# First expert's rows by one-hot products from rows kept on chip, gates applied to its outputs, and a fourth buffer for split q and k

## The chip, the cores and the metric

One Trainium2 chip, one core. The metric is device time in microseconds of one launch. A core has TensorE (PE, matrix products; its weight loads are listed as PEld), VectorE (DVE), ScalarE (ACT), GpSimd (POOL) and SyncE (SP, which here issues transfers); each runs its own instructions in order and they meet by semaphores.

## The reference

Attention for 2 batches, 8 heads, 576 positions, width 64, with a bias from a small network of the positions; a mixture of experts over the 1152 resulting rows; and a gated network over its output. What matters here is the middle part:

```python
logits = x @ w_gate
expert_idx = np.argmax(logits, axis=1)
...
gate_w = probs[np.arange(N), expert_idx]
...
for i in range(N):
    e = expert_idx[i]
    if counts[e] < capacity:
        disp[e, counts[e]] = x[i]
        pos[i] = counts[e]
        counts[e] += 1
        keep[i] = True
h = np.maximum(np.einsum('ecd,edf->ecf', disp, w1), 0.0)
y = np.einsum('ecf,efd->ecd', h, w2)
...
        out[i] = gate_w[i] * y[expert_idx[i], pos[i]]
```

x has 1152 rows of 512, there are 8 experts of 512 x 1024 x 512, and the capacity is 288.

## The kernel before

All large products are done in a 32-bit type that TensorE reads in one pass (fp32r), each operand split into a high part (a copy rounded to that type) and a low part (the rest): high by high, high by low, low by high.

**Attention.** The work is a list of units, nine per head: four tiles of 128 queries of batch 0, one tile of the last 64 queries of both batches, four tiles of batch 1. For each head and batch `load` (line 217) brings q, k and v in one transfer (`raw`, two buffers), and GpSimd splits them: high parts of q and k (L231, two instructions of 640 columns), low part of q (L233), low part of k (L235, the tile K2), high and low part of v (L240, L242). The tiles QK and K2 have three buffers, so a split waits until TensorE is done with the head before last. `LOADS0` and `LOADS` give the units at which the two loads of the next head are issued. Softmaxed scores are multiplied with v; `folds` (L399) turns a head's output by one product per token tile into rows, with the eight gate logits beside them; VectorE divides by the sums (L411), SyncE stores the 64 columns of all 1152 rows into `rows` in device memory (L413), and GpSimd adds up the logits in `lg` (L417, L419).

**Routing.** `route` (L605) works on the 1152 x 8 logits with some thirty small VectorE instructions and a few products. It gives `slot` (L699): for each row its place in the experts' order of size, largest first, counted from a base below zero so that only kept rows match; and then ranks, lists and registers (L702 to L715).

**Experts.** `experts` (line 1062) takes the largest expert first (k = 0, up to 288 rows), then the second. For k = 0: `pick` (L870) makes nine one-hot tiles of 128 tokens x 288 slots in 16 bits, `gather` (L889 to L902) multiplies them with the tokens' numbers and gates (27 products with nine columns each) to get a list of row numbers, and loads these rows from `rows` by three indirect transfers on GpSimd's queue. Then `scale` multiplies each row by its gate, `turn` transposes on TensorE (L937), and ScalarE and VectorE split into `dh` and `dl` (L941, L942). `split` (L962, L963) does the same for the expert's weights, eight pieces of 1024 columns; the first three are loaded as soon as the largest expert is known. `full` (L975) then runs 4 x 24 products for the first layer (L992), with high and low parts of the hidden values (L996, L997), 4 x 24 for the second (L1006), and `evac` writes the outputs' high and low parts into `x2h` and `x2l` (L969, L970), from which the gated network (`swiglu`) reads. Within `full` the steps `around` and `extra` put the next expert's loads, splits and gather, and the narrowing of the gated network's 64-bit weights (L769 to L775), between the pieces. The columns of `x2h` and `x2l` past the first 288 are zeroed by ScalarE (L1152, eight instructions) between routing and the experts. `warm` (L1141) issues products that nobody reads: 16, 12 and 64 of them.

The order on each engine is that in which the code is written (`manual_schedule`); nothing is reordered by a scheduler in the parts shown.

Of the kernel before, what the change touches and what calls it, by code (L numbers as in the profile page):

```python
# [23 lines left out]
NT = 9  # L24
# [26 lines left out]
LOADS0, LOADS = (0, 7), (0, 5)  # L51
# [15 lines left out]
WARM = (16, 12, 64)  # L67
# [77 lines left out]
def build(tc, ins, out, cap):  # L145
    nc = tc.nc
    cap = max(0, min(int(cap), N))
    with ExitStack() as ctx:
# [18 lines left out]
        x_p = ctx.enter_context(tc.tile_pool(name="axh", bufs=2))  # L167
        with ExitStack() as pctx:
            ps = pctx.enter_context(tc.tile_pool(name="ps", bufs=2, space=PSUM))
            attention(tc, ins, cst, rt, lg, x_p, rows, tids, out, ps)  # L170
        moe(tc, ins, cst, cap, rt, lg, x_p, rows, tids, out)


def attention(tc, ins, cst, rt, lg, x_p, rows, tids, out, ps):
    nc = tc.nc
    with ExitStack() as ctx:
# [26 lines left out]
        with ExitStack() as actx:  # L203
            attn_phase(tc, actx, (load, qk, loads), cst, (bias, head), (out, zi), fold, lg, x_p, rows, ps)


def loader(tc, ctx, ins):
# [3 lines left out]
    qk_p = ctx.enter_context(tc.tile_pool(name="aqk", bufs=3))  # L211
# [36 lines left out]
def attn_phase(tc, ctx, load, cst, bias, zeros, fold, lg, x_p, rows, ps):  # L248
# [14 lines left out]
    sco, ex, tp, tt, sums, pt, ot, rsum = {}, {}, {}, {}, {}, {}, {}, {}  # L263
    eps = m_p.tile([128, 1], F32, name="eps", bufs=1)
    V.memset(eps, 1e-9)

# [132 lines left out]
    def folds(h):  # L399
# [5 lines left out]
        for t0, tn in ((0, 5), (5, 4)):  # L405
# [6 lines left out]
            if t0:  # L412
# [71 lines left out]
    assert not pt and not ot  # L484

# [248 lines left out]
def moe(tc, ins, cst, cap, rt, lg, x_p, rows, tids, out):  # L734
# [3 lines left out]
    with ExitStack() as ctx:  # L738
        xp = ctx.enter_context(tc.tile_pool(name="x2", bufs=1))
        x2h = xp.tile([128, 4, XC], F32R, name="x2h")  # L740
        x2l = xp.tile([128, 4, XC], F32R, name="x2l")
# [47 lines left out]
        with ExitStack() as bctx:  # L789
            bctx.enter_context(tc.manual_schedule(engines=ENGINES))  # L790
            kept, rare = experts(tc, bctx, ins, cst, cap, rt, lg, x_p, rows, tids, x2h, x2l, load64, narrow, split)
# [27 lines left out]
class Experts:  # L819


    def __init__(self, tc, ins, cst, rt, pool, pp, x_p, rows, tids, x2h, x2l):
# [23 lines left out]
        self.hl = pool.tile([128, 8, SL], F32R, name="hl")  # L846
        self.eid, self.base = {}, {0: 0}
# [26 lines left out]

    def gather(self, k, few=False):

# [3 lines left out]
        if k == 1:  # L880
            pl = [pp.tile([128, SL], F32, name="pl", tag="py0", bufs=1)]
        else:
            pl = [pp.tile([128, 512], F32, name="pl", tag="ph") for r in range(npart if k == 0 else 1)]
# [486 lines left out]
```

## Time and profile before

| | us |
|---|---|
| median of 3 runs | 447.68 |
| lowest, highest | 446.14, 449.28 |
| profiled execution, its own time | 446.49 |
| its span | 444.6 |
| bias and head 0 | to about 80 |
| heads 1 to 7 | to about 220 |
| routing to the first expert's products | 220 to 243.4 |
| first and second expert | 243.4 to about 302 |
| rest of the experts, gated network | to the end |

Stages and waits are read from one profiled execution, whose times are from the start of its span. Busy time counts instructions, not waiting; the granted clock of TensorE is given as a share of its full level, 2.4 GHz, and the lower level is half of it.

### The profile page before, as it was taken

What the parts mean: (1) busy time and instruction counts of PE and PEld (TensorE: products, weight loads), DVE (VectorE), ACT (ScalarE), POOL (GpSimd) and SP (SyncE); (2) the same over time, 40 slices, a digit from 0 to 9 for tenths busy, and PEclk for the clock granted to TensorE, in tenths of its full rate; (3) what the DMA queues carried; (4) which work ended last, traced back from release to release, by engine and by line L of the source; (5) the groups of instructions that cost most, each with busy time, mean ns of one, the idle gap of its engine ahead of it and who ended that gap; (6) DMA issues with size and microseconds to landing.
All of it is one profiled execution on the core that took longest, in us unless ns stands there. A gap on an engine that the chain in (4) does not pass through costs nothing.

```text
span 444.6 us, 8757 instructions
## 1 busy us (share of the span) xinstructions
PE 396.1 (89%) x3122; PEld 342.5 (77%) x3122; DVE 343.1 (77%) x737; ACT 279.1 (63%) x586; POOL 115.5 (26%) x109
## 2 busy tenths in 40 slices
PE   8786777679999999999986989998989999999993
PEld 5332236569999999998865988996978888888992
DVE  6999987379999999999675578854778888787341
ACT  4888887479989989889591448444354444444221
POOL 0000000898597888960021100010000000000003
PEclk9999899899999999999988899999999999999999
DMA  7555557872955857720294988985444444440003
GB/s 252 206 214 190 183 192 226 269 260 82 287 184 187 241 179 244 232 97 6 57 308 31 331 253 125 351 238 181 143 142 143 142 143 142 143 143 1 1 1 116
DMA packets 54210, 76.35 MB, mean 172 GB/s; under 512 B 16562, under 2 KB 35762, under 8 KB 54160
## 3 DMA queue, kind: packets, MB, share of 16 engines
q1 hardware_dynamic: 51744, 70.62, 50.0%
q0 software_dynamic: 800, 2.48, 3.2%
q10 hardware_dynamic: 1616, 2.62, 1.9%
q8 instruction: 26, 0.43, 0.4%
q14 instruction: 24, 0.20, 0.1%
HBM read 59.13 MB, written 16.59 MB: 170 GB/s over the span
## 4 chain that ended last, share of the span: by engine, by line
PE 44%; DVE 21%; ACT 10%; issue 6%; DMA 5%; POOL 2%; SPq 0%; DVEq 0%; POOLq 0%; ACTq 0%
PE pg L1243 9%; PE tp L334 6%; PE po L381 5%; PE sc L282 5%; PE ph L992 5%; PE py L1006 4%; DVE swl L785 4%; DVE wf L771 4%; PE po L408 3%; DMA bias<-biasd 2%; DVE sg L1251 2%; ACT pth L337 2%; PE pb L569 2%; DMA xr<-rows,ri 2%; ACT ex L314 2%
## 5 line engine op out<-in xcount | busy, mean ns | idle before, releaser
L297 DVE CUSTOM_DVE_ANT_0 ex<-sc,bias 128x576 f32<-128x576 f32 x72 | 53.8, 748 | 9.3 <-PE tt L344 7.0
L231 POOL TENSOR_TENSOR QK<-raw,zero 128x640 fp32r<-128x640 f32 x28 | 34.5, 1254 | 90.6 <-DMA raw<-in_qkv 87.2
L569 PE MATMUL pb<-r,w 128*32 128x288 f32 x576 | 45.2, 424 | 14.4 <-ACT r L563 9.4
L565 DVE TENSOR_SCALAR r<-ltab,sl,nb 128x576 f32<-128x576 f32 x116 | 57.2, 570 | 0.0
L314 ACT ACTIVATE ex<-ex,mx 128x576 f32<-128x576 f32 x72 | 55.8, 775 | 1.4 <-DVE mx L297 0.7
L337 ACT ACTIVATE pth<-tp 128x512 fp32r<-128x512 f32 (+1 forms) x80 | 43.8, 554 | 16.5 <-PE tp L334 7.7
L282 PE MATMUL sc<-QK 128*128 128x288 f32 x160 | 49.1, 324 | 3.6 <-POOL QK L233 3.1
L353 DVE TENSOR_TENSOR ptl<-tp,pth 128x512 fp32r<-128x512 f32 (+1 forms) x80 | 49.6, 628 | 2.3 <-ACT pth L337 1.6
L1243 PE MATMUL pg<-x2h,swh 128*128 128x304 f32 x192 | 46.4, 309 | 4.9 <-DVE sg L1251 4.1
L334 PE MATMUL tp<-cst,ex 128*128 128x128 f32 x288 | 44.6, 278 | 6.2 <-DVE ptl L353 3.8
L569 PEld LDWEIGHTS pb<-r,w 128*32 128x32 f32 x576 | 18.4, 112 | 40.8 <-ACT r L563 22.2
L282 PE MATMUL sc<-K,QK 128*128 128x288 f32 x160 | 45.0, 297 | 1.2 <-POOL K L235 1.2
L1243 PE MATMUL pg<-x2l,swh 128*128 128x304 f32 x192 | 43.9, 303 | 0.0
L381 PE MATMUL po<-pth,W 128*128 128x256 f32 (+1 forms) x145 | 43.6, 321 | 0.0
L1243 PE MATMUL pg<-x2h,swl 128*128 128x304 f32 x192 | 43.6, 301 | 0.0
L1275 POOL DMA_INDIRECT out<-ob,ids x5 | 4.9, 973 | 144.1 <-ACT ob L1272 143.2
L334 PEld LDWEIGHTS tp<-cst,ex 128*128 128x128 f32 x288 | 32.8, 142 | 11.0 <-ACT ex L314 4.6
L1255 ACT ACTIVATE sh<-sg 128x608 fp32r<-128x608 f32 (+1 forms) x13 | 8.8, 673 | 51.2 <-DVE sg L1251 51.2
L1243 PEld LDWEIGHTS pg<-x2h,swh 128*128 128x128 f32 x192 | 32.7, 188 | 9.7 <-DVE sg L1251 7.1
L1251 DVE TENSOR_TENSOR sg<-pg,sg 128x304 f32<-128x304 f32 x48 | 20.7, 468 | 22.1 <-PE pg L1243 18.6
L282 PEld LDWEIGHTS sc<-QK 128*128 128x128 f32 x160 | 30.3, 189 | 5.3 <-POOL QK L233 3.3
L381 PE MATMUL po<-ptl,W 128*128 128x256 f32 (+1 forms) x116 | 33.4, 308 | 0.0
(191 smaller groups left out, 1023.9 us busy)
## 6 DMA issues: line engine op xcount, KB each, us to landing
raw<-in_qkv SPq DMA_DIRECT2D x16, 800.0 KB, 5.7
biasd<-be SPq DMA_DIRECT2D x36, 288.0 KB, 2.2
wr<-in_ew SPq DMA_DIRECT2D x19, 512.0 KB, 8.9
w<-in_mwg SPq DMA_DIRECT2D x12, 512.0 KB, 3.6
w<-in_mwv SPq DMA_DIRECT2D x12, 512.0 KB, 4.7
w<-in_mwo SPq DMA_DIRECT2D x12, 512.0 KB, 6.2
bias<-biasd SPq DMA_DIRECT2D x16, 288.0 KB, 4.1
bias<-biasd SPq DMA_DIRECT2D x17, 256.0 KB, 4.3
```

The source lines that it names most:

```text
L231: P.tensor_tensor(QK[:, o:o + n], raw[:, o:o + n], view(zero, 0, (0, n)), op=ALU.add)
L282: nc.tensor.matmul(sc[:, c, :288], l, K[:, o + c * 288:o + (c + 1) * 288], start=n == 0, stop=n == len(lhs) - 1)
L297: V.tensor_tensor_reduce(e.rearrange("p (c j) -> p c j", c=2), sc[:, :, :288], head[h][:, t].rearrange("p (c j) -> p c j", c=2), scale=-0.125,
L314: A.activation(ex[u], ex[u], AF.Exp, bias=mx, scale=-1.0, accum_out=sums[h][:, col:col + 1])
L334: nc.tensor.transpose(x[:, kt], e[:, kt * 128:(kt + 1) * 128], ident)
L337: A.activation(hi[:, :4, c], x[:, :, o], AF.Copy)
L353: V.tensor_tensor(lo[:, :, c], x[:, :, o], hi[:, :4, c].bitcast(F32), op=ALU.subtract)
L381: nc.tensor.matmul(po[:, :w], W[:, kt], src[:, kt, a:a + w], start=k == 0, stop=k == 8)
L565: V.tensor_scalar(r[g], x, s, nb, op0=ALU.mult, op1=ALU.max)
L569: nc.tensor.matmul(pb[strips[g], c, :288], w2, r[g][:, c * 288:(c + 1) * 288], start=True, stop=True, skip_group_check=True,)
L1243: nc.tensor.matmul(g[:, :TB], w[:, a * 4 + kk], x[:, kk, c0 + b * TB:c0 + (b + 1) * TB], start=kk == 0 and i == 0, stop=kk == 3 and i == 2,)
L1251: V.tensor_tensor(sg[:, cs], g[:, :TB], sg[:, cs], op=ALU.mult)
```

## The change

`x2h` and `x2l` are now made ahead of attention. GpSimd zeroes their columns past 1152 at the start, and after each head `folds` keeps that head's 64 columns of all rows in them, token tiles by 128 partitions, as a high and a low part: on GpSimd for heads 0 to 6, and for head 7 the high part on ScalarE and the low part later on VectorE (`late`). ScalarE's eight zeroing instructions go. `dispatch` makes nine one-hot tiles in fp32r (in the tiles `hh` and `hl`, not yet in use) and multiplies them with the kept rows, 72 products, which gives the first expert's rows transposed, without gate; `halve` is the old end of `turn`. The 27 products for the row numbers and gates of the first expert are still done, its row loads, scaling and transposes are not. `spread` puts the gates into all partitions (three products and a copy), and at the end of the first `full` VectorE multiplies the four output tiles by them. The second expert's gather moves from ahead of `full` to its second piece. QK and K2 get a fourth buffer; head 1's second load is issued at unit 4 of head 0 instead of 7; the warming products are 16 and 24.

```diff
-LOADS0, LOADS = (0, 7), (0, 5)
+LOADS0, LOADS = (0, 4), (0, 5)
...
-WARM = (16, 12, 64)
+WARM = (16, 24)
...
-    qk_p = ctx.enter_context(tc.tile_pool(name="aqk", bufs=3))
+    qk_p = ctx.enter_context(tc.tile_pool(name="aqk", bufs=4))
...
+    for x in x2:
+        nc.gpsimd.memset(x.rearrange("p d c -> p (d c)")[:, NT * DM:].bitcast(F32), 0.0)
+    xhi, xlo = tokens(x2)
...
+                to = slice(h * D, h * D + D)
+                if h == H - 1:
+                    A.activation(xhi[:, :, to], x, AF.Copy)
+                    late.append((xlo[:, :, to], x, xhi[:, :, to].bitcast(F32)))
+                else:
+                    nc.gpsimd.tensor_tensor(xhi[:, :, to], x, view(nil, 0, (0, NT), (0, D)), op=ALU.add)
+                    nc.gpsimd.tensor_tensor(xlo[:, :, to], x, xhi[:, :, to].bitcast(F32), op=ALU.subtract)
...
+    def dispatch(self, late):
+
+        nc, V, rt = self.nc, self.nc.vector, self.rt
+        sel = [self.hh[:, t] for t in range(8)] + [self.hl[:, 0]]
+        for t in range(NT):
+            V.tensor_scalar(sel[t], rt["iota"], rt["slot"][:, t:t + 1], None, op0=ALU.is_equal)
+        V.tensor_tensor(*late, op=ALU.subtract)
+        tp = [self.pp.tile([128, 512], F32, name="etp", tag="ph")[:, :SL] for d in range(4)]
+        x = tokens(self.x2)
+        for dd in (range(3), (3,)):
+            for t in range(NT):
+                for d, n in [(d, n) for n in range(2) for d in dd] if t + 1 < NT else [(d, n) for d in dd for n in range(2)]:
+                    nc.tensor.matmul(
+                        tp[d], x[n][:, t, d * 128:(d + 1) * 128], sel[t], start=t == n == 0, stop=t == NT - 1 and n == 1
+                    )
+        return tp
+
+    def spread(self):
+
+        nc = self.nc
+        g = self.pp.tile([128, 512], F32, name="g", tag="ph")[:, :SL]
+        for r, (o, w) in enumerate(self.parts):
+            x = self.li[0][:w, r, 2:3]
+            ones = bass.AP(tensor=x.tensor, offset=x.offset, ap=[list(x.ap[0]), [0, 128]])
+            nc.tensor.matmul(g[:, o:o + w], ones, self.ident[:w, :w], start=True, stop=True)
+        nc.scalar.activation(self.gb, g, AF.Copy)
...
-        for r, (o, w) in enumerate(parts):
+        for r, (o, w) in enumerate(parts if k else ()):
             nc.gpsimd.indirect_dma_start(
...
+        if k == 0:
+            for x in py:
+                nc.vector.tensor_tensor(x, x, self.gb, op=ALU.mult)
         self.evac(b, py, SL)
...
+                if k == 0 and c == 1:
+                    x.gather(n)
+                if k == 0 and c == 2:
+                    x.spread()
...
-    for t in (x2l, x2h):
-        for d in range(4):
-            A.activation(t[:, d, SL:], view(cst, 0, (0, XC - SL)), AF.Copy, scale=0.0)
     x.eid[0] = x.reg("first", 0, 0, E - 1, SP + ACT)
     for q in range(Q1):
         x.load(q)
     next(routing)
+    tp = x.dispatch(late)
+    x.split(0)
+    next(routing)
     x.pick(0)
+    x.halve(tp)
     x.gather(0)
-    warm(WARM[2])
-    next(routing)
-    x.split(0)
+    x.split(1)
     x.pick(1)
-    x.split(1)
-    for r in range(npart):
-        x.scale(0, r, vector=r < npart - 1)
     kept = x.reg("regs", 0, 0, N)
-    x.turn(0, lambda: x.gather(1))
```

The order on VectorE, from the end of the routing's lists to the first low part of hidden values of the first expert. Before (sel are the 16-bit one-hots, wl the low part of a weight piece, xr the loaded rows, pl and li the list of row numbers and gates, dl the low part of the turned rows):

```order
L715 CAST regs<-list 1x33
L963 TENSOR_TENSOR wl_3180<-wr_3171,wh_3179 128x1024
L866 TENSOR_SCALAR rel<-slot,list 128x9
L870 TENSOR_SCALAR sel<-iota,rel 128x288 x9
L963 TENSOR_TENSOR wl_3182<-wr_3172,wh_3181 128x1024
L916 TENSOR_SCALAR xr_3191<-xr_3191,li_3187 96x512
L916 TENSOR_SCALAR xr_3192<-xr_3192,li_3187 96x512
L851 TENSOR_LOAD regs
L895 TENSOR_REDUCE li_3188<-pl 96x9
L899 CAST ri_3190<-li_3188 96x3
L900 TENSOR_SCALAR li_3188<-li_3188 96x3
L942 TENSOR_TENSOR dl<-etp,dh 128x288 x4
```

Of the changed kernel, the same stretch of VectorE (L893 is the old L870, L989 the old L942, L1009 the old L963, L1043 the old L997):

```order
L737 CAST regs<-list 1x33
L893 TENSOR_SCALAR sel<-iota,slot 128x288 x9
L989 TENSOR_TENSOR dl<-etp,dh 128x288 x4
L938 TENSOR_REDUCE li_3209<-pl 96x9
L942 CAST ri_3211<-li_3209 96x3
L943 TENSOR_SCALAR li_3209<-li_3209 96x3
L1009 TENSOR_TENSOR wl_3204<-wr_3194,wh_3203 128x1024
L889 TENSOR_SCALAR rel<-slot,list 128x9
L893 TENSOR_SCALAR sel<-iota,rel 128x288 x9
L874 TENSOR_LOAD regs
L1009 TENSOR_TENSOR wl_3206<-wr_3195,wh_3205 128x1024
L1043 SCALAR_TENSOR_TENSOR hl<-ph,hh 128x288 x2
```

The first expert's one-hots moved from ahead of the ranks to behind them, the turned rows' low parts moved ahead of the second weight split, and the second expert's one-hots now stand behind that split, ahead of the third. Just before this stretch VectorE of the changed kernel has the one-hots in fp32r, the late low part and the first weight split ahead of the ranks:

```order
L721 TENSOR_REDUCE slot<-hs 128x9
L903 TENSOR_SCALAR hh<-iota,slot 128x288 x8
L903 TENSOR_SCALAR hl<-iota,slot 128x288
L904 TENSOR_TENSOR x2l<-xh,x2h 128x9x64
L1009 TENSOR_TENSOR wl_3202<-wr_3193,wh_3201 128x1024
L724 TENSOR_REDUCE rank<-hs 128x8
```

Where the first 16-bit one-hots stood directly behind the slots, the first weight split now stands ahead of the ranks, so everything behind it waits for that weight piece.

On GpSimd, between the second load of a head and the first load of the next but one, here with head 1's rows. Before (raw is the loaded q, k and v, lg the sum of the logits, xh a head's rows and logits):

```order
L235 TENSOR_TENSOR K_1565<-raw,QK 128x640
L240 TENSOR_TENSOR W<-raw,zero 128x5x64
L242 TENSOR_TENSOR W<-raw,W 128x5x64
L419 TENSOR_TENSOR lg<-lg,xh 128x72
L231 TENSOR_TENSOR QK<-raw,zero 128x640 x2
```

Of the changed kernel, the same place:

```order
L242 TENSOR_TENSOR K_1576<-raw,QK 128x640
L247 TENSOR_TENSOR W<-raw,zero 128x5x64
L249 TENSOR_TENSOR W<-raw,W 128x5x64
L433 TENSOR_TENSOR lg<-lg,xh 128x72
L439 TENSOR_TENSOR x2h<-xh,nil 128x9x64
L440 TENSOR_TENSOR x2l<-xh,x2h 128x9x64
L238 TENSOR_TENSOR QK<-raw,zero 128x640 x2
```

Two instructions of 576 columns came in between the addition of the logits and the next load's splits; nothing else moved.

## Rows read from the trace of the kernel before

**Rows 1.** The page: span of the profiled execution, us, and its instructions.

```profile
span 444.6 us, 8757 instructions
```

**Rows 2.** Busy us by stretch (instructions): PE, PEld, DVE, ACT, POOL; PEclk, DMA share, GB/s.

```profile
179.42:196.63 17.21, 17.06 (x137) 16.50 (x136) 15.91 (x43) 15.75 (x45) 14.43 (x14) 1.00 0.54 167
224.00:226.00 2.00, 0.31 (x4) 0.11 (x3) 1.83 (x11) 2.00 (x3) 0.00 (x0) 1.00 1.11 399
228.00:231.00 3.00, 3.00 (x16) 2.06 (x14) 1.75 (x11) 3.00 (x4) 1.43 (x2) 0.50 1.01 326
236.00:240.00 4.00, 1.04 (x9) 0.56 (x7) 1.53 (x3) 0.00 (x0) 0.00 (x0) 1.00 0.57 34
240.00:243.40 3.40, 2.64 (x36) 2.26 (x36) 0.93 (x5) 1.68 (x5) 0.48 (x1) 0.74 0.07 25
243.40:248.40 5.00, 5.00 (x21) 5.00 (x22) 2.69 (x6) 1.72 (x4) 2.42 (x3) 0.50 0.80 261
248.40:255.00 6.60, 6.60 (x51) 6.60 (x51) 4.22 (x15) 3.54 (x6) 0.00 (x0) 1.00 1.05 330
```

**Rows 3.** Chain of waits, 219 to 276: start us, us, what it went through.

```profile
225.28 0.24 DVE slot L699
232.00 9.12 DMA xr<-rows,ri
243.40 8.89 PE ph L992 x48
```

**Rows 4.** Instructions in time, 226 to 244: start, us, engine, line, operation, output<-inputs, count.

```profile
228.26 0.21 DVE L702 TENSOR_REDUCE rank<-hs 128x8 f32<-128x64 f32 x1
229.75 0.17 DVE L715 CAST regs<-list 1x33 int32<-1x33 f32 x1
233.60 1.93 DVE L870 TENSOR_SCALAR sel<-iota,rel 128x288 bf16<-128x288 f16 x9
240.39 1.34 PE L889 MATMUL pl<-ids,sel 128*96 128x9 bf16 x27
242.89 1.55 DVE L942 TENSOR_TENSOR dl<-etp,dh 128x288 fp32r<-128x288 f32 x4 [0.66 <-ACT dh L941]
```

**Rows 5.** First weight loads (224 to 233), then the split of weights (all): ns min/median/max.

```profile
L953 SPq DMA_DIRECT2D wr<-in_ew x3: 368/373/397, 224.8 to 226.0; - x3
DMA to landing us min/median/max: 6.1/6.7/7.3
...
L962 ACT ACTIVATE wh<-wr x16: 1039/1047/1086, 231.1 to 292.9; 128x1024 fp32r<-128x1024 f32 x16
L963 DVE TENSOR_TENSOR wl<-wr,wh x16: 1211/1222/1226, 232.2 to 295.8; 128x1024 fp32r<-128x1024 f32 x16
```

**Rows 6.** Instructions in time in the first expert; in brackets idle before, and its releaser.

```profile
259.35 1.58 ACT L773 ACTIVATE w<-w 128x1536 f32<-128x1536 f32 x1 [3.46 <-DVE wf L771]
...
263.18 0.40 PE L1006 MATMUL py<-hh,wl 128*128 128x288 f32 x1 [0.85 <-DVE wl L963]
...
268.67 1.32 ACT L918 ACTIVATE xh<-xh,li 96x512 f32<-96x512 f32 x2
...
275.65 1.54 DVE L970 TENSOR_TENSOR x2l<-py,x2h 128x288 fp32r<-128x288 f32 x4
```

**Rows 7.** Instructions in time, GpSimd loading heads 5 to 7, and TensorE's first use.

```profile
157.20 2.46 POOL L231 TENSOR_TENSOR QK<-raw,zero 128x640 fp32r<-128x640 f32 x2 [2.94 <-DMA raw<-in_qkv]
...
173.28 2.46 POOL L231 TENSOR_TENSOR QK<-raw,zero 128x640 fp32r<-128x640 f32 x2 [1.05 <-PE sc L282]
...
180.90 2.46 POOL L231 TENSOR_TENSOR QK<-raw,zero 128x640 fp32r<-128x640 f32 x2
...
185.09 1.57 POOL L235 TENSOR_TENSOR K<-raw,QK 128x640 fp32r<-128x640 f32 x1
...
187.41 0.89 POOL L242 TENSOR_TENSOR W<-raw,W 128x320 fp32r<-128x320 f32 x1
...
191.81 0.38 PE L282 MATMUL sc<-QK 128*128 128x288 f32 x1
```

More of the change, by code (lines that the diff above doesn't have):

```diff
@@ L167, in build, with tokens, attention @@
         x_p = ctx.enter_context(tc.tile_pool(name="axh", bufs=2))
+        xp = ctx.enter_context(tc.tile_pool(name="x2", bufs=1))
+        x2 = [xp.tile([128, 4, XC], F32R, name=f"x2{x}") for x in "hl"]
         with ExitStack() as pctx:
             ps = pctx.enter_context(tc.tile_pool(name="ps", bufs=2, space=PSUM))
-            attention(tc, ins, cst, rt, lg, x_p, rows, tids, out, ps)
-        moe(tc, ins, cst, cap, rt, lg, x_p, rows, tids, out)
-def attention(tc, ins, cst, rt, lg, x_p, rows, tids, out, ps):
+            late = attention(tc, ins, cst, rt, lg, x_p, x2, rows, tids, out, ps)
+        moe(tc, ins, cst, cap, rt, lg, x_p, x2, late, rows, tids, out)
+def tokens(x2):
+    return [x.rearrange("p d c -> p (d c)")[:, :NT * DM].rearrange("p (t c) -> p t c", t=NT) for x in x2]
+def attention(tc, ins, cst, rt, lg, x_p, x2, rows, tids, out, ps):
     nc = tc.nc
@@ L203, in attention @@
         with ExitStack() as actx:
-            attn_phase(tc, actx, (load, qk, loads), cst, (bias, head), (out, zi), fold, lg, x_p, rows, ps)
+            return attn_phase(tc, actx, (load, qk, loads), cst, (bias, head), (out, zi), fold, lg, x_p, x2, rows, ps)
 def loader(tc, ctx, ins):
@@ L245, in loader, with attn_phase @@
     return load
-def attn_phase(tc, ctx, load, cst, bias, zeros, fold, lg, x_p, rows, ps):
+def attn_phase(tc, ctx, load, cst, bias, zeros, fold, lg, x_p, x2, rows, ps):
     nc = tc.nc
@@ L484, in attn_phase @@
     assert not pt and not ot
+    return late[0]
 def prepare(nc, pool, ins, rt, tids):
@@ L733, in route, with moe @@
     yield
-def moe(tc, ins, cst, cap, rt, lg, x_p, rows, tids, out):
+def moe(tc, ins, cst, cap, rt, lg, x_p, x2, late, rows, tids, out):
     nc = tc.nc
@@ L790, in moe @@
             bctx.enter_context(tc.manual_schedule(engines=ENGINES))
-            kept, rare = experts(tc, bctx, ins, cst, cap, rt, lg, x_p, rows, tids, x2h, x2l, load64, narrow, split)
+            kept, rare = experts(tc, bctx, ins, cst, cap, rt, lg, x_p, rows, tids, x2h, x2l, late, load64, narrow, split)
         def last():
@@ L846, in __init__ @@
         self.hl = pool.tile([128, 8, SL], F32R, name="hl")
+        self.gb = self.xrs[0][1][:, :SL]
         self.eid, self.base = {}, {0: 0}
@@ L927, in turn_few, with turn @@
         self.nc.scalar.activation(self.xs, tp.rearrange("p (d n) -> p d n", d=4), AF.Copy)
-    def turn(self, k, between=None):
+    def turn(self, k):
         nc, V, dh, dl = self.nc, self.nc.vector, self.dh, self.dl
@@ L933, in turn @@
         for r, (o, w) in enumerate(self.parts):
-            if r == len(self.parts) - 1 and between:
-                between()
             for d in range(4):
@@ L1059, in second, with experts @@
     return sorted(fd, key=lambda x: x[1]) if c == 7 else fd
-def experts(tc, ctx, ins, cst, cap, rt, lg, x_p, rows, tids, x2h, x2l, load64, narrow, split2):
+def experts(tc, ctx, ins, cst, cap, rt, lg, x_p, rows, tids, x2h, x2l, late, load64, narrow, split2):
     nc = tc.nc
```

43 lines of the change are left out of this document (20 added, 23 removed).

## Prediction

> **What bounds the kernel now.** I read the page first: the span of the profiled execution is 444.6 us [rows 1], and that run took 446.49 us, so 1.9 us lie around the span. Then the busy time by stage. In the attention heads TensorE is the limit: in one head of 17.21 us it is busy 17.06 [rows 2]. Between the last head and the first expert it is not: from 224.0 to 226.0 it works 0.31 us, from 236.0 to 240.0 1.04 us. Its granted clock is at the lower of its two levels (1.2 of 2.4 GHz) from 228 to 231 and from 243.4 to 248.4; in the latter stretch 21 products of 288 columns take 5.00 us, 0.238 each, against 51 in 6.60 us, 0.129 each, behind it. So I read the chain of waits there [rows 3]: the slots are known at 225.28 + 0.24 = 225.5; the chain then runs to a row load of 9.12 us (232.00 to 241.1) and reaches the first expert's products at 243.40, of which 48 end 8.89 us later, at 252.29. The reader is to see that 18 us pass between knowing the slots and the first product, half of them one indirect load, and that the products behind it start at half clock.
>
> **What replaces the load, and which wait comes next.** The rows of the first expert now come out of 72 products (nine token tiles, four quarters, high and low part). They have the shape of the expert's own: 72 x 0.129 = 9.3 us. The first one-hot is ready about 0.4 us behind the slots, and 24 warming products lead up to it, so they run from 225.9 to 235.2. The nine one-hots in this type are nowhere in the trace: from 0.21 each (1.93 for nine in 16 bits, [rows 4]) to 0.34 (288 of the 1024 32-bit columns that take 1.22, [rows 5]). With the late low part (576 columns, four of 288 take 1.55: 0.8) they end by 225.5 + 3.1 + 0.8 = 229.4 at the latest. What stands next on VectorE waits until 232.0, so I cost them at nothing; without that cover they would cost 1.9 + 0.8 at least.
>
> That next wait is the weights. The order puts the first split of weights ahead of the ranks and of the second set of one-hots. Its load is issued at 224.8 and the three loads land in 6.1 to 7.3 us [rows 5]; I take 6.1 for the first: 230.9. ScalarE's half 1.04 -> 232.0, VectorE's 1.22 -> 233.2. The seven small routing instructions (228.26 to 229.92, [rows 4]: 1.66, 0.24 each) -> 234.9. The nine one-hots 1.93 -> 236.8. TensorE, which ended its 72 products at 235.2, runs the 27 nine-column products that wait for them (1.34 for all; the last 18 can only follow: 0.9) -> 237.8. The low parts (1.55 for four) need until 238.4, but the first product needs only the first. So the expert starts at 237.8, not 243.40: **5.6 us earlier**. If the weights land sooner the bound is the 72 products: 235.2 + 1.34 + 0.1 = 236.6; if the first takes 7.3 us it is 239.0.
>
> **What the first expert loses and gains.** Its first 24 products now run at 0.129: 3.1 us, to 240.9. Before the second 24 stands the second expert's 27 products, which need VectorE: low parts to 238.4, three small instructions (0.24 each) 239.1, second weight split 240.3, one subtraction and nine one-hots 242.5, then 0.9 -> 243.4. That is a new wait of 1.6 us and 0.9 of work. 24 more products: 246.5, where it was 252.29: **5.8 us earlier**. The missing half clock (2.3 us for 21 products) pays for this. From there the trace shows a chain that TensorE waits for: small routing instructions, the narrowing of the gate weights on VectorE, on ScalarE a scaling that idled 3.46 us for it, the sixth weight split, and the product that waits 0.85 us for that at 263.18 [rows 6]. It hangs on the 48th product, so it moves as a whole: 257.4. TensorE gets there with 0.4 us of gate products and 9.3 us of others at 256.2, in time. So the gates' products are hidden; without that cover they cost their 0.4.
>
> The second expert's row load is issued later relative to the products (its list follows the 27 products and a weight split, about 246.5, three issues, then at most the 9.12 us seen: about 259.5); the scaling that needs it stood at 268.67 [rows 6], so at 262.9 now: hidden, with 3.4 us to spare.
>
> At the expert's end four multiplications by the gates come on VectorE, 288 columns from PSUM, like the low parts there (1.54 for four, [rows 6]); the last can only follow the last product, so VectorE reaches the next weight split 0.4 to 1.9 us later. What later waits of VectorE absorb of this can't be read from one row, so the bounds are 0 and 1.9 lost; I take 0.4, the part that stands behind the last product whatever else VectorE does.
>
> **What attention pays.** GpSimd gets two instructions of 576 columns in six heads that matter. At its rate for 640 columns (2.46 for two additions, 1.57 for a subtraction, [rows 7]) that is 1.1 + 1.4 = 2.5 us; at the rate of 320 strided ones (0.89) 1.6 each, 3.2. I take 2.6, since the rows read and written are as long as those of the latter but the count is nearer the former. They stand behind a head's second load. The place that could hurt is the last head: its K ends at 185.09 + 1.57 = 186.66 and is first used at 191.81, 5.15 us of room. GpSimd's last wait for a load ahead of that, 2.94 us before 157.20, still soaks up the pairs before it; two pairs lie behind it, and the fourth buffer takes away GpSimd's wait of 1.05 for TensorE at 173.28: 2 x 2.6 - 1.05 = 4.15 late, so 1.0 us is left. Cost 0 (0 at 2.5, 0.2 at 3.2). The buffer itself gains nothing: none of TensorE's waits there is for one. ScalarE's copy of the last head (576 of the 1024 columns that take 1.04: 0.6) lies ahead of an exponential that waits for VectorE anyway.
>
> **Sum.** 446.49 - 5.8 + 0.4 = 441.1 us. The profiled run is 1.2 us below the median of the runs shown (447.68, from 446.14 to 449.28); the runs of the changed kernel will scatter likewise, so I say 441.5.
>
> **Rivals.**
> *The clock falls again.* After 235.2 TensorE runs only nine-column products or waits until 237.8, and again from 240.9 to 243.4. In the trace the clock fell after 1.04 us of work in 236.0 to 240.0 and nine-column products behind it (0.74 of full in 240.0 to 243.4, [rows 2]); the 2.6 us here are shorter, which speaks against it. At 0.238 the first 24 products take 5.7 us, to 243.5; the wait for VectorE is then over, so 0.9 + 3.1 -> 247.5: 1.0 us lost, 442.5. If the second 24 run so too, 2.6 more: 445.1. The Trainium skill, page "TensorE: Matmul & The Clock Gate", section "HAM oscillation — how this bites in real kernels", says that waits between bursts of matmuls let the clock drop, burst after burst; by that rule it would be the 445.1. The trace agrees that it can happen here (the two stretches above), not that it must.
> *The weights were there earlier.* The landing of 6.1 us may be that of another of the three loads. Then the products set the start, 1.2 us sooner: 440.3.
> *VectorE falls behind in the experts.* It has the one-hots, splits and multiplications now in a shorter stretch. With the full 1.9 us and another 1 us in the first expert: 443.6.
> *Slower: GpSimd becomes the bound of attention.* Its place is the last head's K. With p for a pair, the room ends at 2p - 1.05 = 5.15, p = 3.1. Above that up to five pairs push it, so 5.4 us of gain are eaten at p = 3.1 + 5.4/5 = 4.2, and at 5.0 the kernel ends at 441.1 + 9.5 = 450.6. Against it: every GpSimd row of that shape gives 3.2 at most.
> *The load was hidden anyway* I give nothing: the chain of waits runs through it.
>
> **Chances.** The forecast 0.47 (alone 440 to 443), the clock 0.22 (442.5 more often than 445.1), weights 0.13, VectorE 0.12, GpSimd 0.06. The range leaves out the last and the worst of the clock: 439.0 to 445.2. A measurement of this kernel tells about 1% from no change, so faster means under 443.2: nearly all of the forecast and of the weights, half of the clock, a third of VectorE: 0.72; within 1% 0.24; slower 0.04.
>
> **What would show it.** Right: the first expert product near 237.8 at full clock with the weight split just ahead of it in the chain; 27 nine-column products waiting for VectorE near 242; the 48th product near 246.5; GpSimd's last K before its first use. Wrong: dispatch products at 0.238, TensorE waiting for GpSimd in heads 5 to 7, or the stall near 257 grown beyond the 0.85 us it has.

## The result, and the profile after

The changed kernel takes 442.46 us (median of eight runs, 440.11 to 443.81) against 447.51 us (eight runs, 446.14 to 450.76) of the kernel before in the same comparison. The medians lie 1.1% apart; the ratio of the two on record, which is not the quotient of the medians, is 0.9864, 95% interval 0.9836 to 0.9893. So the kernel is 1.1 to 1.4% faster. The forecast was 441.5, in a range of 439.0 to 445.2. Its profiled execution took 440.11 us, the lowest of the eight; the sum of the prediction, made against the profiled execution of before, gave 441.1.

The page, where [rows 1] stood:

```profile
span 437.9 us, 8781 instructions
```

The stretches of [rows 2] in the changed kernel, with the same columns: busy us (instructions) of PE, PEld, DVE, ACT, POOL; granted clock, DMA share, GB/s.

```profile
179.42:196.63 17.21, 17.07 (x138) 16.50 (x136) 16.10 (x43) 15.74 (x45) 16.66 (x16) 1.00 0.56 168
224.00:226.00 2.00, 1.56 (x14) 1.18 (x13) 1.86 (x9) 0.00 (x0) 0.00 (x0) 1.00 1.04 387
228.00:231.00 3.00, 3.00 (x24) 3.00 (x24) 0.58 (x1) 0.69 (x1) 0.00 (x0) 1.00 0.95 319
236.00:240.00 4.00, 4.00 (x43) 3.91 (x44) 3.93 (x15) 2.12 (x4) 0.00 (x0) 1.00 0.66 221
240.00:243.40 3.40, 3.40 (x41) 3.09 (x40) 3.40 (x10) 1.53 (x3) 0.00 (x0) 1.00 0.92 315
```

TensorE's 1.04 us of work in 236.0 to 240.0 has become 4.00, and the granted clock, which was 0.50 from 228 to 231 and 0.74 from 240 to 243.4, is 1.00 in all of them. In attention one number moved much: GpSimd is busy 16.66 us in a head of 17.21, not 14.43.

The chain of waits where [rows 3] stood (start us, us, what it went through):

```profile
225.04 0.24 DVE slot L721
225.73 9.83 PE etp L910 x72
235.56 1.56 PE pl L934 x27
237.12 3.28 PE ph L1038 x24
240.40 1.77 PE pl L934 x27
242.18 3.29 PE ph L1038 x24
...
261.36 3.31 PE py L1052 x23
...
268.87 7.14 PE ph L1038 x54
```

The row load of 9.12 us is gone from it. Instead it is all TensorE from 225.73 to 245.47. In the two traces the first expert product is 6.3 us earlier (237.12 for 243.40), the 48th ends 6.8 us earlier (245.47 for 252.29), the second expert starts 6.7 us earlier (268.87 for 275.60), and at the gated network's first product 6.3 us are left (302.67 for 308.93). The slots, on which all of this waits, are known 0.24 us earlier in this execution, which can't be put down to the change; against the slots it is 6.0, 6.6, 6.5 and 6.0 us.

The other side, weights and VectorE, instructions in time (in brackets idle before and its releaser), for [rows 4], [rows 5] and [rows 6]:

```profile
230.31 1.06 ACT L1008 ACTIVATE wh<-wr 128x1024 fp32r<-128x1024 f32 x1 [7.75 <-DMA wr<-in_ew]
...
231.40 1.23 DVE L1009 TENSOR_TENSOR wl<-wr,wh 128x1024 fp32r<-128x1024 f32 x1 [2.82 <-ACT wh L1008]
...
234.14 1.91 DVE L893 TENSOR_SCALAR sel<-iota,slot 128x288 bf16<-128x288 f16 x9
...
239.17 1.93 DVE L893 TENSOR_SCALAR sel<-iota,rel 128x288 bf16<-128x288 f16 x9
...
268.92 1.55 DVE L1062 TENSOR_TENSOR py<-py,xr 128x288 f32<-128x288 f32 x4
```

And GpSimd in the last heads, with TensorE's first use of the last head's K, for [rows 7]:

```profile
122.81 2.46 POOL L238 TENSOR_TENSOR QK<-raw,zero 128x640 fp32r<-128x640 f32 x2 [2.62 <-DMA raw<-in_qkv]
...
165.60 1.14 POOL L439 TENSOR_TENSOR x2h<-xh,nil 128x576 fp32r<-128x576 f32 x1
...
183.19 1.15 POOL L439 TENSOR_TENSOR x2h<-xh,nil 128x576 fp32r<-128x576 f32 x1
184.42 1.43 POOL L440 TENSOR_TENSOR x2l<-xh,x2h 128x576 fp32r<-128x576 f32 x1
...
189.98 1.56 POOL L242 TENSOR_TENSOR K<-raw,QK 128x640 fp32r<-128x640 f32 x1
...
191.66 0.33 PE L296 MATMUL sc<-K,QK 128*128 128x288 f32 x1
```

From 122.81 to the last split GpSimd has no idle time that the trace shows. The last head's K is split at 191.54 and used at 191.66: of the 1.0 us of room in the prediction 0.1 is left. And GpSimd's heads stand 17.59 us apart (165.60 and 183.19), TensorE's 17.21. So with the pairs GpSimd is the slower of the two by 0.4 us per head, and room that is used up doesn't come back; its 16.66 us of busy time in a window of 17.21 don't show that, since the gaps of under 0.1 us between its instructions count as neither busy nor waiting.

### The profile page after: what moved, and what is told of

Its sections match the earlier page's. It is cut to its first block, busy times and chain, and to the rows that moved or that the text cites. A ratio compares the mean times of both kernels' runs of the same rounds, so it can differ in the third digit from the quotient of the medians.

```text
span 437.9 us, 8781 instructions
## 1 busy us (share of the span) xinstructions
PE 395.4 (90%) x3136; PEld 344.2 (79%) x3136; DVE 345.7 (79%) x747; ACT 270.9 (62%) x579; POOL 131.2 (30%) x122
## 4 chain that ended last, share of the span: by engine, by line
PE 42%; DVE 21%; ACT 10%; DMA 7%; issue 6%; POOL 2%; SPq 1%; DVEq 0%; ACTq 0%; POOLq 0%
PE pg L1290 9%; PE tp L348 5%; PE po L395 5%; PE sc L296 5%; DMA wr<-in_ew 4%; DVE swl L806 4%; DVE wf L792 4%; PE ph L1038 4%; PE pb L591 3%; PE po L422 3%; ACT pth L351 2%; PE etp L910 2%; DVE sg L1298 2%; ACT ex L328 2%; DMA bias<-biasd 2%
## 5 line engine op out<-in xcount | busy, mean ns | idle before, releaser
L587 DVE TENSOR_SCALAR r<-ltab,sl,nb 128x576 f32<-128x576 f32 x116 | 57.3, 592 | 0.3 <-PE pb L591 0.2
L351 ACT ACTIVATE pth<-tp 128x512 fp32r<-128x512 f32 (+1 forms) x80 | 43.7, 553 | 16.3 <-PE tp L348 8.3
L395 PE MATMUL po<-pth,W 128*128 128x256 f32 (+1 forms) x145 | 43.7, 322 | 0.0
```

Of the source, the lines that this page charges most:

```text
L351: A.activation(hi[:, :4, c], x[:, :, o], AF.Copy)
L395: nc.tensor.matmul(po[:, :w], W[:, kt], src[:, kt, a:a + w], start=k == 0, stop=k == 8)
L587: V.tensor_scalar(r[g], x, s, nb, op0=ALU.mult, op1=ALU.max)
```

## Experiments

Each is compared with runs of the kernel before on its own chip (three chips in all), where that kernel's median was 448.7 to 450.4 us, higher than in the first comparison; so kernels with the change are read against the changed kernel (442.46 above; 442.40, 439.16 to 444.11, six runs, when it was run again beside the last three). On the other two chips the changed kernel was not run itself, so a difference of 1 us there shows little. Ratios and their intervals are those on record and not quotients of the medians. One more thing has to be known for all of them: the instant at which the slots are known differs by 2.9 us between two profiled executions of the changed kernel itself (225.04 and 227.90; where it comes from stands below, under the changed kernel again). What lies behind the slots is therefore read from the slots on.

### Attention: what the buffer and GpSimd's pairs do

**Three buffers.**

```
-    qk_p = ctx.enter_context(tc.tile_pool(name="aqk", bufs=4))
+    qk_p = ctx.enter_context(tc.tile_pool(name="aqk", bufs=3))
...
-LOADS0, LOADS = (0, 4), (0, 5)
+LOADS0, LOADS = (0, 7), (0, 5)
```

> The changed kernel with three buffers for the split q and k instead of four, and the second load of head 1 issued at its old place. Theory (the buffer gains nothing, as the prediction said): in the kernel before, GpSimd waited for TensorE at 139.20 and 173.28 because a buffer was not free; with the pairs it reaches the same splits at 140.38 and 175.56, later than the buffers come free, so the waits do not come back. Time as with four buffers, 442.5 us, GpSimd's waits together under 1 us, last head's K ending near 191.5. Rival (the buffer is what makes room for the pairs): waits of 1 to 2 us come back in two heads, the last head's K ends at 193 to 194, TensorE waits for it as long, and the time is 444 to 445 us.

Measured: 442.64 us (440.38 to 444.47). GpSimd's waits in attention (engine, line, what for: us, times, longest):

```profile
POOL QK L238 <- DVE ptl L367: 77.1, 1, 77.1
POOL QK L238 <- DMA raw<-in_qkv: 3.2, 1, 3.2
POOL lg L431 <- DVE xh L425: 2.0, 1, 2.0
```

The 77.1 us are the time before its first load. Of the waits for TensorE (2.23 at 139.20, 1.05 at 173.28 in the kernel before) none came back. The last head's K ends at 193.84, 2.3 us later than in the changed kernel, but GpSimd was 2.3 us later from its wait for a load on (125.07 for 122.81), and 125.75 is what the changed kernel shows when run again. So with the pairs in place the fourth buffer does nothing that shows. The prediction said that it gains nothing, but also put down the 1.05 us at 173.28 as room that it makes for the pairs; this run shows that the pairs take up that wait by themselves, with three buffers too.

**The attention part alone**, in the kernel before: fourth buffer, the earlier load, pairs, ScalarE's copy of the last head; the rows still come by the indirect load.

> The kernel before with the attention part of the change alone: the fourth buffer, the pairs on GpSimd, the last head's copy on ScalarE; the first expert's rows still come by the indirect load. Theory: all of the gain is behind the slots, so this is as the kernel before, 447.5 us, within 0.5. Rival (the fourth buffer helps attention): faster, 446 us or less. Rival (the pairs cost something that the rest of the change repays): slower, 448.5 us or more.

Measured: 449.84 us against 450.41, ratio 0.9997 (0.9952 to 1.0043). Attention by itself gained and lost nothing that can be measured; the slots stand at 225.80 in its trace, at 225.28 in that of before. The trace shows one thing more: the last of the three row loads took 10.6 us from issue to landing here, where [rows 3] has 9.12, and the first expert product came 20.5 us behind the slots, not 18.1. So the load that the change removes is not the same in every execution, and [rows 3] shows a short one.

**Without the pairs.**

```
-                    nc.gpsimd.tensor_tensor(xhi[:, :, to], x, view(nil, 0, (0, NT), (0, D)), op=ALU.add)
-                    nc.gpsimd.tensor_tensor(xlo[:, :, to], x, xhi[:, :, to].bitcast(F32), op=ALU.subtract)
+                    pass
...
-        nc.gpsimd.memset(x.rearrange("p d c -> p (d c)")[:, NT * DM:].bitcast(F32), 0.0)
+        nc.gpsimd.memset(x.rearrange("p d c -> p (d c)").bitcast(F32), 0.0)
```

> The changed kernel without GpSimd's two instructions per head that write the rows' high and low parts; the kept rows are zeros but for the last head, so this part of the computation is left out. Theory (the pairs are hidden by the room of the last head's K): 442.5 us, as the changed kernel, within 0.3 us in the profile up to the slots. Rival (the pairs push GpSimd onto the path): faster by 1 us or more, and the slots are known over 1 us earlier.

Measured: 448.51 us, 6 us slower, which neither theory had. The edit brought a cost of its own: GpSimd now clears the whole of both tiles, 5760 columns each, where the changed kernel clears the last 1152 of them. The first 40 us of this kernel, and then those of the changed kernel (columns as in the windows above):

```profile
0.00:40.00 40.00, 28.07 (x306) 12.55 (x310) 35.47 (x65) 24.23 (x35) 10.53 (x8) 0.91 0.54 192
```

```profile
0.00:40.00 40.00, 31.15 (x358) 14.83 (x358) 35.66 (x77) 28.91 (x43) 2.76 (x8) 1.00 0.64 226
```

While GpSimd is busy for 10.53 us instead of 2.76, VectorE finishes 65 instructions instead of 77 in nearly the same busy time, and head 0's first score product comes at 72.45, not at 66.85. Without these 5.6 us it is 442.9. From that product to the slots it takes 160.3 us here, 158.2 and 161.1 us in the two executions of the changed kernel: no gain from the missing pairs that stands out of their own difference. The run answers the question only through this subtraction.

**A dearer pair.** The first instruction of the pair twice (a pair then takes 3.8 us), and the whole pair twice (5.2 us).

> The changed kernel with the first of GpSimd's two instructions done twice in each head: a pair costs 3.8 us instead of 2.6. By the prediction's sum (room for 3.1 us a pair, up to five pairs behind that): 3.5 us more, 446. By the trace of the changed kernel (GpSimd works without a gap from 122.81 on, four pairs lie between that and the last head's K, whose split ends 0.1 us before its first use): 4 x 1.2 - 0.1 = 4.7 us more, 447.2, and TensorE waits for GpSimd in the last heads. Rival (room is left): no more than 1 us.

> The changed kernel with GpSimd's two instructions done twice in each head: a pair costs 5.2 us. By the prediction's sum: 5 x (5.2 - 3.1) = 10.5 us more, 453. By the trace of the changed kernel: 4 x 2.6 - 0.1 = 10.3 us more, 452.8. If GpSimd is the bound, TensorE's head lasts as long as GpSimd's: 17.6 + 2.6 = 20.2 us. Rival (TensorE still sets the pace): under 3 us more.

Measured: 446.0 us (444.91 to 447.55), 3.6 more, and 453.39 us, 11.0 more (two runs). What TensorE waits for in heads 2 to 7 of the first:

```profile
141.19 0.40 PE L296 MATMUL sc<-K,QK 128*128 128x288 f32 x1 [0.21 <-POOL K L242]
160.01 0.40 PE L296 MATMUL sc<-K,QK 128*128 128x288 f32 x1 [1.23 <-POOL K L242]
178.82 0.40 PE L296 MATMUL sc<-K,QK 128*128 128x288 f32 x1 [1.23 <-POOL K L242]
197.63 0.40 PE L296 MATMUL sc<-K,QK 128*128 128x288 f32 x1 [1.23 <-POOL K L242]
```

These stand 18.8 us apart, and GpSimd's own heads 18.8 too (its first pair instructions at 169.19 and 188.00): TensorE runs at GpSimd's pace. The price is what the prediction's sum gave (3.5 and 10.5), but the agreement of the first is in part luck. The sum had five pairs that lose 0.7 each above a limit of 3.1; the trace has heads of 18.8 us, 1.6 above TensorE's 17.2, in three heads and 0.3 in one. Between the two runs the gain of 5 us is used up at a pair of about 4.1 us, where the rival had put 4.2. So that rival was right in its mechanism and close in its price, and 1.5 us per pair away from eating the whole gain; that GpSimd sets the pace begins much sooner, at a pair of 2.6 us (the changed kernel again, below).

### Behind the slots: products, clock, gates

**The clock alone**, in the kernel before.

```
-WARM = (16, 12, 64)
+WARM = (16, 12, 94)
```

> The kernel before with 94 instead of 64 warming products behind the first list: TensorE then works until about 239.7 instead of 236.5, in the time in which it waits for the indirect load; nothing else is changed. Theory (the low clock of 243.4 to 248.4 is a term of its own in the gain): the first expert's products run at 0.13 us each from the first, the 48th product ends 2.3 us earlier, at about 250.0, and the time is 2.0 to 2.3 us below the kernel before. Rival (another engine holds the first expert anyway, the clock is worth nothing): 0 to 0.5 us. In either case the first expert product stays near 243.4.

Measured: 446.82 us against 448.73, ratio 0.9979 (0.9947 to 1.0011). The first expert's 24 products, the first at 245.51, in this kernel:

```profile
245.51:248.67 3.16, 3.16 (x24) 3.16 (x25) 1.33 (x4) 1.36 (x4) 2.45 (x3) 1.00 0.77 252
```

The last of the row loads, for which ScalarE waits in this kernel:

```profile
243.44 0.72 ACT L918 ACTIVATE xr<-xr,li 96x512 f32<-96x512 f32 x1 [9.31 <-DMA xr<-rows,ri]
```

The products take 0.13 us each, where 21 took 0.238 in [rows 2]. The first of them came 1.1 us later from the slots (19.2 for 18.1 us), but not because of the extra warming products, which ended at 242.0: the last row load was issued at 233.24 and landed at 243.4, 10.1 us later and not 9.12 (the attention part alone, without extra warming products, shows 10.6), and the last transposes waited for its scaling until 244.21. From the first product to the second expert it is 2.3 us less (29.8 for 32.0), from the slots 1.2 us less (49.0 for 50.2). So the clock is a term of its own, about 2.3 us by the trace, of which this execution lost half again to a longer load; the time itself can't tell the gain from none.

**Half the products.**

```
-                for d, n in [(d, n) for n in range(2) for d in dd] if t + 1 < NT else [(d, n) for d in dd for n in range(2)]:
+                for d, n in [(d, 0) for d in dd]:
...
```

> The changed kernel with 36 instead of 72 products for the first expert's rows: the low parts of the rows are left out of them, and the first expert computes with the high parts alone. Theory A (VectorE stands right behind the products: its one-hots for the first list end at 236.05): the products end at 230.6, the first expert product comes at about 236.4 instead of 237.12, the second list is paced by VectorE as before, and the time falls by only 0.3 to 0.5 us. Theory B (the 72 products are the bound by themselves): they are paid in full, 4.9 us less. Theory C (the 72 products are also what holds the clock up): TensorE waits 5 us, the clock is at the lower level when the expert starts, 21 products cost 0.24 us each, and the time is 1.5 to 2 us more than the changed kernel's.

Measured: 443.0 us (441.38 to 445.17). Chain and windows of this kernel, whose slots are known at 226.5:

```profile
235.54 3.32 PE pl L934 x27
238.86 5.32 PE ph L1038 x24
244.18 1.18 PE pl L934 x27
245.36 3.27 PE ph L1038 x24
```

```profile
231.00:234.00 3.00, 1.22 (x10) 0.98 (x8) 1.49 (x3) 2.62 (x6) 0.00 (x0) 1.00 0.49 170
234.00:236.00 2.00, 0.46 (x3) 0.29 (x3) 1.90 (x10) 0.59 (x1) 0.00 (x0) 1.00 0.00 0
236.00:240.00 4.00, 4.00 (x30) 3.60 (x31) 3.64 (x14) 1.06 (x1) 0.00 (x0) 0.55 0.71 251
240.00:243.40 3.40, 3.40 (x17) 3.40 (x16) 3.36 (x12) 0.41 (x1) 0.00 (x0) 0.52 1.02 360
```

By the trace it is theory C: 4.9 us of TensorE's work less, and from the slots to the second expert 1.8 us more (45.5 for 43.7). The time itself, 0.5 us above the changed kernel's 442.46, shows neither a gain nor a loss. TensorE worked 1.68 us in the 5 us from 231 to 236, and the clock stood at its lower level from about 236 on: 27 list products took 3.32 us instead of 1.56, 24 expert products 5.32 instead of 3.28. The list products started 1.5 us earlier from the slots (9.0 us for 10.5), not 4.9: TensorE had waited 3.32 us for VectorE's first one-hots, which stand right behind the products (theory A).

This is the rival of the prediction in which the clock falls again, in another kernel. The Trainium skill, page "TensorE: Matmul & The Clock Gate", section "HAM oscillation — how this bites in real kernels", says that waits between bursts of matmuls let the clock drop; this trace agrees. In the changed kernel TensorE works without a gap there, and the clock stays at 1.00.

**Without the gates.**

```
-            for x in py:
-                nc.vector.tensor_tensor(x, x, self.gb, op=ALU.mult)
...
-                if k == 0 and c == 2:
-                    x.spread()
```

> The changed kernel without the gates of the first expert: the six products that spread them, their copy and the four multiplications are left out, so the first expert's outputs are not scaled. Theory of the prediction: 0.4 us less than the changed kernel (442.1). From the trace of the changed kernel: the 1.5 us of multiplications were absorbed before the second expert's last weight split, so 0.0 to 0.2 less (442.4). Rival (the multiplications delay the second expert's splits in full): 1.5 to 1.9 us less (440.7).

Measured: 442.49 us (440.52 to 443.12), as with them. In this trace the low parts of the outputs start at 268.86 and the weight split that waits longest for ScalarE in the second expert stands at 286.23, 0.2 and 17.6 us behind that expert's first product (268.64). In the changed kernel the low parts start at 270.38, 1.7 us behind that product (268.70), and the split at 286.29, 17.6 us behind. Without the gates, then with them:

```profile
268.86 1.54 DVE L1016 TENSOR_TENSOR x2l<-py,x2h 128x288 fp32r<-128x288 f32 x4
...
286.23 1.22 DVE L1009 TENSOR_TENSOR wl<-wr,wh 128x1024 fp32r<-128x1024 f32 x1 [2.27 <-ACT wh L1008]
```

```profile
270.38 1.54 DVE L1016 TENSOR_TENSOR x2l<-py,x2h 128x288 fp32r<-128x288 f32 x4
...
286.29 1.23 DVE L1009 TENSOR_TENSOR wl<-wr,wh 128x1024 fp32r<-128x1024 f32 x1 [2.27 <-ACT wh L1008]
```

VectorE waits 2.27 us for ScalarE there in either kernel: the time of the four multiplications has been made up by then, and they cost 0.

### The small expert, and two further edits

**The changed kernel again.**

> The changed kernel itself once more, beside the three edits of it below, on their chip: 442.5 us (440 to 444).

Measured: 442.40 us (439.16 to 444.11), ratio 0.9838 (0.9785 to 0.9891) on this chip. TensorE's waits for K in the later heads of its profiled execution:

```profile
159.41 0.40 PE L296 MATMUL sc<-K,QK 128*128 128x288 f32 x1 [0.28 <-POOL K L242]
177.00 0.40 PE L296 MATMUL sc<-K,QK 128*128 128x288 f32 x1 [0.27 <-POOL K L242]
194.58 0.40 PE L296 MATMUL sc<-K,QK 128*128 128x288 f32 x1 [0.27 <-POOL K L242]
```

They stand 17.6 us apart, GpSimd's own pace. This is part of what puts the slots at 227.90 here and not at 225.04. Of the 2.9 us, 0.6 stand at the start of head 1 (GpSimd starts on its load at 79.32, not 78.72) and 1.9 at its end, with a granted clock of 0.79 from 98 to 106, where it was 1.00; the last 1.0 is lost behind that, where GpSimd, whose load came at 125.75 and not at 122.81, holds TensorE in three heads.

**Lists first.** VectorE makes the routing lists and the first one-hots in the time in which it waited for weights.

```
     tp = x.dispatch(late)
-    x.split(0)
     next(routing)
+    next(routing)
     x.pick(0)
+    x.split(0)
...
             yield from (None,) * Y0
-            next(routing)
```

> The changed kernel with the first weight split on VectorE moved behind the routing lists and the first one-hots, and the last eleven small routing instructions (2.1 us, 246.39 to 248.48 in the changed kernel) moved up with the lists, into the 2.8 us in which VectorE waited for the first weights. Theory (from the trace of the changed kernel): the expert's start does not move, since TensorE is busy without a gap up to it (72 products to 235.56, 27 list products to 237.12); the chain behind the 48th product is 2.1 us shorter, and the time falls by 1.5 to 2.1 us, to 440.7. Theory of the prediction (the weights' split is what the start waits for): the start comes 0.5 us or more earlier too, and the time falls by 2.5 us or more. Rival (the chain behind the 48th product is set by ScalarE or by the weights' loads): under 0.5 us.

Measured: 443.48 us (441.46 to 444.46), no gain. From the slots it is 11.6 us to the first expert product, as in the changed kernel (11.5 and 11.9): TensorE, not the weights' split, sets the start. To the second expert it is 41.0 us instead of 43.2 and 43.7: the 2.1 us of the moved instructions were gained, and 0.1 to 0.5 more. Then this, in the same trace (a wait in the small expert, and the first products of the gated network):

```profile
300.59 0.64 PE L1090 MATMUL py<-wr,hs 128*32 128x128 f32 x16 [1.00 <-DMA wr<-in_ew]
```

```profile
302.81:311.50 8.69, 8.69 (x51) 8.69 (x52) 4.12 (x6) 2.75 (x5) 0.00 (x0) 0.80 0.05 3
```

The small expert waits 1.0 us for its last weights, and the gated network starts at the lower clock: 51 products in 8.69 us. That clock is not this edit's. The changed kernel's wait there (first fence: its profiled execution; second: the execution when run again), and the stretch behind it:

```profile
300.45 0.64 PE L1090 MATMUL py<-wr,hs 128*32 128x128 f32 x16 [0.32 <-DMA wr<-in_ew]
...
302.67:311.00 8.33, 8.33 (x59) 8.33 (x60) 4.67 (x7) 3.37 (x6) 0.00 (x0) 1.00 0.13 11
```

```profile
303.02 0.64 PE L1090 MATMUL py<-wr,hs 128*32 128x128 f32 x16 [0.51 <-DMA wr<-in_ew]
...
305.23:314.00 8.77, 8.77 (x52) 8.77 (x53) 4.21 (x7) 2.78 (x5) 0.00 (x0) 0.81 0.05 3
```

The kernel before has no such wait: its 64 products ran at a stretch from 305.35. In all nine profiled executions with the change and without the next edit the wait is there, 0.3 to 1.4 us long. The clock fell behind it in four (waits of 0.51, 1.00, 1.25, 1.32) and not in five (0.32, 0.41, 0.55, 0.59, 1.38), so its length alone doesn't decide.

**Loads later.**

```
             yield from narrow(1)
+        else:
             load64(3)
-        else:
             yield from narrow(2, 0, N2)
```

> The changed kernel with the loads of the fourth slice of the gate weights (three of 512 KB) issued behind the last weight load of the small expert instead of ahead of it. Theory: the 0.5 us that the changed kernel loses in the small expert (its second product waits for a load issued at 290.93 that lands at 300.41) come back: 442.0, and no wait for weights in the small expert. Rival (the landing is set by all transfers together, not by the order of issue): no change.

> Both edits of the two kernels named lists first and loads later. Theory: the gains add, 2.0 to 2.6 us below the changed kernel, 440.2; with the lists alone the small expert would wait longer for its last weights and keep less of the gain. Rival (the loads hold the small expert in any order): no better than the lists alone, or no better than the changed kernel.

Measured: 440.56 us (439.13 to 443.17) for the loads alone, 440.99 us (437.72 to 443.96) for both. The small expert with the loads later, and with both:

```profile
298.45 1.95 PE L1090 MATMUL py<-wr,hs 128*32 128x128 f32 x64 [0.47 <-ACT hs L1084]
```

```profile
302.14:311.00 8.86, 8.86 (x63) 8.86 (x64) 5.03 (x8) 3.88 (x7) 0.00 (x0) 1.00 0.19 39
```

The wait is gone in both, and the clock stays up. Read from the slots (start of the row that makes them) in each profiled execution, us to:

| kernel | first expert product | second expert | gated network | last output issued |
|---|---|---|---|---|
| before | 18.1 | 50.2 | 83.7 | 213.9 |
| changed | 11.9 | 43.7 | 77.6 | 208.0 |
| changed, again | 11.5 | 43.2 | 77.3 | 209.1 |
| lists first | 11.6 | 41.0 | 75.7 | 207.4 |
| loads later | 11.5 | 43.2 | 76.7 | 207.0 |
| both | 11.5 | 41.0 | 74.4 | 204.8 |

In the traces the two edits together gain 3.2 to 4.3 us between the slots and the last output (204.8 for 208.0 and 209.1). In the medians, six runs each, they don't show: 440.56 and 440.99 against 442.40, in spreads of 4 to 6 us that overlap. That either beats the changed kernel is likely from the traces and not shown by the times.

## Why the prediction was right, step by step

**The start: 237.8 forecast, 237.12 measured.** Close in its number, not right in its bound. The prediction put the start down to VectorE's chain: first weights, split, routing instructions, one-hots. The first weights were split by ScalarE from 230.31, 5.7 us behind their issue (6.1 taken), and every step behind it came 0.6 to 0.9 us sooner, 0.24 of it from the slots: VectorE's half at 231.40, one-hots ended at 236.05 (236.8). The products in turn took 9.83 us, 0.137 each, not 0.129, to 235.56 (235.2), and from there TensorE had no gap up to the first expert product. So TensorE's own work set the start, and VectorE at most the 0.4 us by which the 27 list products were stretched to 1.56 in this execution; in others (without the gates, with either dearer pair) they took 1.18 us. Moving VectorE's order (lists first) did not move the start. That the forecast came out within 0.7 us is in part luck: a chain that was sized too long was close to products that were sized too short. The rival in which the weights are there earlier had the path right, and its 236.6 lacked 0.5 us, most of it the products' price.

**The 48th product: 246.5 forecast, 245.47 measured.** The wait for VectorE ahead of the second 24 products was taken too long: the second one-hots ended at 241.1, not 242.5, since the low parts were done 0.9 us sooner (237.5) and three small instructions took 0.35 us in a row, not 0.7. The wait of 1.6 us and 0.9 of work became 27 products in 1.77 us. This term and the start were each sized 0.7 us too long; the two times 24 products, 6.6 us and not 6.2, gave 0.4 back. That leaves 1.0 us.

**The chain behind it** moved as a whole, as said: 6.8 us at the 48th product, 6.7 at the second expert. From the slots to the last output the two executions of the changed kernel take 5.9 and 4.8 us less than that of the kernel before; the sum had 5.4 (5.8 less the 0.4 of the gates). That VectorE could have shortened it by 2.1 us was not seen.

**The clock** stayed up, the likelier case. What the prediction put down as 2.3 us for 21 products is right in size (2.0 for 24 with half the products, 2.3 with the clock alone). That it is the 72 products that keep it up is what half the products shows: with 36 of them it fell.

**The gates** cost 0 instead of 0.4: within the bounds, the slack was there.

**The second expert's load** was hidden: issued from 245.47 on, its scaling at 261.94 waited for nothing.

**Attention** cost nothing that the trace shows in the profiled execution, and the pair took 2.6 us as forecast. The room came out at 0.1 us instead of 1.0, though the sum over the pairs held: four pairs (10.4 us) took up GpSimd's three waits of the kernel before (2.23, 2.94 and 1.05), which leaves 4.2 us late, where the prediction had 4.15. What ate the room is that GpSimd's load came 0.9 us later (122.81 for 121.95) and that TensorE was 0.4 us ahead (K used at 191.66 for 192.03). The prediction also misread a row: what stands at 191.81 in [rows 7] is the first use of QK, and K is first used 0.2 us later. What it left out is the pace. With the pairs GpSimd's head takes 17.6 us and TensorE's 17.2, so a load that lands late is no longer made up for: when the kernel was run again, TensorE waited for K in three of the last heads, which took 17.6 us each, 1.1 us together that the forecast didn't have. Whether attention as a whole got slower by it is not shown: from the end of head 1 to that of head 7 (the fold products) it takes 103.5 and 104.5 us in the two executions of the changed kernel, 104.0 in that of the kernel before, which has a longer head of its own (17.84).

**A slip in the rivals.** The time for VectorE falling behind, 443.6, is counted from the sum (441.1), those for the clock and the weights from the forecast (441.5); from the latter it would be 444.0.

**Missed**: the small expert's last weights. Their load is issued as much earlier as everything else (290.93 for 297.66), but lands 9.5 us behind its issue; in the kernel before it was needed 9.2 us behind, and nobody waited. In the changed kernel's chain of waits it stands as:

```profile
290.93 9.48 DMA wr<-in_ew
```

It cost 0.5 us in the profiled execution (64 products in 2.48 us, not 2.01); in the other 0.65 and, at the lower clock, about 1.4 (52 products in 8.77 us, where 59 took 8.33). Such losses, and slots that come later than in the profiled execution, may be what separates the median (442.46) from that execution (440.11); the runs without a profile can't show it. Why the load takes longer there is open: it stands behind three loads of 512 KB on its queue, and issuing these later removes the wait, but the order was the same in the kernel before.

## What to carry to other kernels

A gather through memory can be replaced by products with one-hot columns even where they are more work for TensorE, if TensorE only waits meanwhile: here 9.8 us of products and 1.6 of lists took the place of 18 us, and kept the clock up for what follows. When a stage moves earlier, look in the trace for each load that was just in time behind it, and for the engine whose spare time pays for the move: here a load with no room cost back 0.5 us in one execution and about 2.1 with the clock in another, and GpSimd was left with 0.1 us and a head 0.4 us longer than TensorE's. Compare such an engine with the one that sets the pace by how far its repeats stand apart, not by its busy share. Taking work away from TensorE can make the stage longer (1.8 us in one trace here), when what is left is a wait.

## What the runs showed of the hardware beyond what was expected

- One-hot columns of 288 in the type that the products take cost VectorE 0.29 us each (eight in 2.33 us), between the 0.21 and 0.34 taken as bounds.
- With 9.9 us of clearing on GpSimd at the start (4.98 and 4.90) the instructions that VectorE ran beside it were slower: 116 instructions of 128 x 576 took 61.7 us instead of 57.3, and the start grew by 5.6 us; nothing else differs that early in the two kernels. The changed kernel's own clearing is 2.1 us long, and its 116 took 57.3 against 57.2 before.
- After a wait of 0.3 to 1.4 us in the small expert the clock was at its lower level in four of nine executions; among those where it stayed up was the longest wait (1.38).
- The last of the three indirect row loads took 9.1, 10.1 and 10.6 us from issue to landing in the three profiled executions that still have it for the first expert.
